# Gated linear attention and a maxout layer: small constants built on the chip, the output matrix read in 3 KB rows, and another order of the work

## The chip, the core and the metric

The kernel runs on one core of a Trainium2 chip. A core has TensorE (PE, with its weight loads shown as PEld), VectorE (DVE), ScalarE (ACT), GpSimd (POOL) and SyncE (SP), which here issues all DMA transfers. The metric is the device time of one execution in microseconds (us).

## The reference

Four batches of 8 heads, 768 tokens, head dimension 48. Each head carries a state of 48x48 from token to token; its rows are decayed by alpha, and the token's key and value are added. The result, 3072 rows of 384, goes through a layer that takes the largest of three products and multiplies it by an output matrix.

```python
for t in range(S):
    state = alpha[:, :, t, :, None] * state + einsum('bhd,bhe->bhde', k[:, :, t], v[:, :, t])
    y[:, :, t] = einsum('bhd,bhde->bhe', q[:, :, t], state)
x = y.transpose(0, 2, 1, 3).reshape(B * S, H * D)           # 3072 x 384
h = maximum(maximum(x @ w1, x @ w2), x @ w3)                # w: 384 x 768
out = h @ w_out                                             # w_out: 768 x 384
```

Inputs and output are float32.

## The kernel before

**Steps.** The work is cut into 12 steps of 256 tokens: step s is chunk s // 4 of batch s % 4. Of a step, partition p holds tokens 2j and 2j+1 of every head (U = 2 halves of J = 64 pairs, R = 2 tokens a pair). A state passes from step s to s + 4.

**One step, in pieces.** Each piece is a function, named by a letter in the order string; the number behind it is a part, then the engine (v DVE, p POOL, a ACT), then @step, and after # the PSUM banks.

- l0 to l3 (L100) load alpha, k, q, v of a step (384 KB each) into rings of four buffers (ra, rk, rq, rv). m (L204) multiplies the pair's two alphas; N (L207) takes the logarithm into la; r0 and r1 (L211) make the inverse decay inside the pair; u and w (L218, L221) bring k and q to the pair's end.
- c (L227) sums logarithms on PE with the triangular matrix upto and the two-column matrix pick; e, f, g (L243 to L249) turn the sums into factors ic, ac and the gates ge by exponentials.
- k and q (L262, L265) scale k and q into qk (float16), V (L268) scales v into vt, v (L273) copies halves of vt to vu.
- T with t (L279, L286) transposes qk on PE with the identity matrix and copies it out of PSUM; D (L289) does the same by DMA, for steps 5 to 11. A (L294) makes the scores, a (L312) masks them into lat with pmask, or with rowmask for step 0.
- Y (L366) applies scores and old state to the values, x (L369) copies the result to xT. S (L378) makes the step's addition to the state, s, M and z (L396, L373, L403) add and decay it, y (L408) spreads it to st.

**The layer.** The maximum is computed as w1 x plus the larger of 0, (w2-w1) x and (w3-w1) x. d (L416) makes the differences wdif in column groups of 256; b (L422) makes w1 in float16, B and n (L425, L431) transpose it, C (L434) makes w_out in float16, P and p (L437, L442) multiply w1 by w_out once into w1o. G (L445) makes the six products of a step with wdif (6 matmuls each), h (L455) takes their maximum into hT, O (L486 in project) multiplies xT by w1o and hT by w_out (9 matmuls), o (L493) scales by ys_c into ob, W (L497) stores.

**Weights in borrowed buffers.** K0 to K8 (L114) load 384 KB pieces of w1, w2, w3, the first eight into buffers 2 and 3 of the input rings; so l0@2, the load of step 2's alpha into ra2, must wait until d0, d1 and b0 have read K0 from it. K9 to K11 load w_out (L121) in rows of 1.5 KB.

**Constants.** Two matrices are computed on the host and loaded as J1 and J0 (L128): ca (34.5 KB: upto, pick and three columns of scales vs_c, ys_c, undo_c) and cb (64 KB: identity and pmask). I (L307) spreads pmask to rowmask.

**Padding.** Heads are 64 wide in las, qks, vts and vus but hold 48 columns; clear_padding (L145) zeroes the rest and the state buffers st: 16 memsets of st and 2 of la on DVE, 3 of vu, 4 of qk and 4 of vt on POOL.

**The order.** The program is one hand-held list, ORDER, which gives each engine its instructions in that order; no scheduler changes it. SP's queue takes loads, stores and DMA transposes in the same order, and one that has to wait holds up all behind it. H pieces (L505) are warm matmuls: products of a zero matrix that fill PE at the start; "H2^k0@1" begins with a small one that waits for the named result (L524). The list begins:

```python
l0@0 J1@0 l1@0 J0@0 l3@0 l0@1 r0a@0 m0v@0 l2@0 N0a@0 r1a@0 u0v@0 H15@0#0 c0@0#0 g0a@0 e0a@0 K0@0 f0a@0
k0v@0 l1@1 V0v@0 K2@0 H6@0#1 H1^k0@0#1 S0@0#1,2 K1@0 l2@1 I0a@0 r0a@1 m0p@1 l3@1 M0p@0 N0a@1 w0v@0 q0v@0
```

Of the kernel before, what the change touches and what calls it, by code (L numbers as in the profile page):

```python
# [23 lines left out]
def kernel(  # L24
# [101 lines left out]
    rowmask = cpool.tile([P, R, P], FP16, name="rowmask")  # L126

    def load_const(_, i, eng):  # L128
        c, c_np = ((ca, ca_np), (cb, cb_np))[i]
        queues[eng].dma_start(c, nc.inline_tensor(c_np, name=f"c{i}").ap())  # L130

    half = ca.bitcast(FP16)
    upto, pick = half[:, :P], half[:, P:P + 2 * U]
    c32 = ca[:, P // 2 + U:]
    ident, pmask = cb[:, :P], cb[:, P:2 * P]
    vs_c, ys_c, undo_c = c32[:, 0:1], c32[:, 1:2], c32[:, 2:3]
# [6 lines left out]
    sts = [[cpool.tile([P, HP, 2, D], FP16, name=f"st{b}_{i}") for i in range(2)] for b in range(B)]  # L143

    def clear_padding():  # L145
        for st in (st for pair in sts for st in pair):
            for i in range(2):
                nc.vector.memset(st[64 * i:64 * (i + 1), :, 1 - i], 0.0)
        for la in las:
            nc.vector.memset(la.rearrange("p r a b c -> p (r a b) c")[:, :, D:], 0.0)  # L150
        for vu in vus:
            nc.gpsimd.memset(vu.rearrange("p u a b c -> p (u a b) c")[:, :, D:], 0.0)
        for qk, vt in zip(qks, vts):
            nc.gpsimd.memset(qk.rearrange("p r i a b c -> p (r i a b) c")[:, :, D:], 0.0)
            nc.gpsimd.memset(vt.rearrange("p a b c -> p (a b) c")[:, :, D:], 0.0)


# [69 lines left out]
    def sums(s, *_):  # L227
# [79 lines left out]
    def spread_mask(_, i, eng):  # L307
        for u in range(U):
            for r in range(R):
                copy(eng, rowmask[u * J:(u + 1) * J, r], pmask[r * J:(r + 1) * J])  # L310

    def masked(s, x, eng):  # L312
# [103 lines left out]
    def differ(_, i, eng):  # L416
        jg, g = divmod(i, 2)
        engines[eng].tensor_sub(  # L418
            wdif[:, :, g, column_group(jg)], staged(3 * jg + 1 + g).rearrange("p (f j) -> p f j", f=NF),
            staged(3 * jg).rearrange("p (f j) -> p f j", f=NF))  # L420
# [101 lines left out]
    def warm_after(n, name):  # L522
# [5 lines left out]
        "l": load_step, "J": lambda _, i, eng: load_const(0, 1 - i, eng), "I": spread_mask, "K": load_weight, "H": warm,  # L528
# [9 lines left out]
    def emit(order):  # L538
# [12 lines left out]
        l0@0 J1@0 l1@0 J0@0 l3@0 l0@1 r0a@0 m0v@0 l2@0 N0a@0 r1a@0 u0v@0 H15@0#0 c0@0#0 g0a@0 e0a@0 K0@0 f0a@0  # L551
        k0v@0 l1@1 V0v@0 K2@0 H6@0#1 H1^k0@0#1 S0@0#1,2 K1@0 l2@1 I0a@0 r0a@1 m0p@1 l3@1 M0p@0 N0a@1 w0v@0 q0v@0
        H6@0#3 c0@1#3 l0@4 f0a@1 H1@0#4 T1@0#4 s0v@0 z0v@0 b0v@0 e0a@1 t1a@0 u0v@1 k0v@1 H1@0#5 B0@0#5 T0@0#6
        y0a@0 r1a@1 d1v@0 t0a@0 d0v@0 g0a@1 n0a@0 H1@0#7 H2^k0@1#7 H0^d1@0#7 A1@0#7,0 A0@0#1,4 w0v@1 l0@2 a2v@0
        K3@0 q0p@1 V0a@1 K4@0 a0v@0 K5@0 s1v@0 a3v@0 l1@2 H3@0#6 H2^a2@0#6 S0@1#6,3 s0a@1 m0p@4 a1v@0 v1a@1
# [5 lines left out]
        A1@2#5,4 V0a@2 l0@5 G4@0#0 a3v@2 a2v@2 A0@2#6,3 b2a@0 S0@2#2,1 M0p@4 M0p@2 G5@1#4 s0v@2 m0p@3 v1a@2
        a1v@2 l2@4 G4@1#5 a0v@2 z0p@2 h4a@0 v0v@2 y0a@2 G5@0#2 h1v@1 Y2@2#3 Y0@2#6 x0v@2 N0a@3 Y3@2 B2@0#0 l1@3
        x1a@2 c0@3#7 M1v@0 C2v@0 n2a@0 G4@2#6 G1@2#3 u0v@4 C0a@0 m0p@5 h5v@0 G3@2#0 l2@3 s1v@2 G2@2#2 C1v@0
        f0a@3 h4a@1 z1v@0 P0@0#1 h2v@2 h3v@2 P1@0#5 l3@4 k0p@4 N0a@5 h5v@1 r0a@3 P2@0#2 h4v@2 p0a@0 l3@3 r1a@3
        p1a@0 c0@5#0 p2v@0 G0@2#4 e0a@5 O1@0#6 h0a@2 g0a@5 w0v@4 q0v@4 e0a@3 T1@4#1 g0a@3 u0v@3 O0@1#5 o1a@0
        k0v@3 l0@7 y1a@0 l1@5 w0v@3 f0a@5 l0@8 r0a@5 q0v@3 T0@4#2 o0a@1 G5@2#4 t1a@4 M1v@1 V0v@4 l0@6 T0@3#7
        V0v@3 O0@0#6 t0a@3 h1v@2 v0p@3 l3@5 t0v@4 h5v@2 S0@4#0,5 v0p@4 o0a@0 S0@3#1,7 s0v@4 A0@4#3,2 s0v@3 l3@6
        T1@3#4 M0v@3 a1v@4 z0p@4 O0@2#6 l1@6 t1a@3 a0v@4 s1v@4 z0p@3 y0a@3 s1v@3 W1@0 m0p@7 A1@4#0,1 y0a@4
        A1@3#2,4 a2v@3 A0@3#3,5 a1v@3 O1@2#7 a3v@4 r0a@7 m0p@6 N0a@7 a3v@3 V0a@5 l2@5 u0p@5 c0@7#2 l2@6 O1@1#5
        N0a@6 r1a@5 a2v@4 v1p@3 l0@9 a0v@3 v1a@4 Y0@4#1 o1v@1 k0p@5 m0p@8 Y3@3#4 Y0@3#0 Y2@3 o0v@2 x0a@3 Y1@4  # L570
        W0@0 Y3@4#3 Y2@4 x1a@3 r0a@6 f0a@7 x0v@4 x1v@4 c0@6#5 G4@3#6 N0a@8 W0@2 w0v@5 G4@4#0 z1v@1 e0a@7 q0v@5
        f0a@6 r1a@6 w0p@6 D0@5 e0a@6 g0a@7 G0@4#4 h0a@4 G2@3#1 h2v@3 G3@3#3 V0a@6 r0a@8 G1@4#2 m0p@9 h4v@3 l2@7
        D1@5 c0@8#4 h3v@3 G5@3#1 q0p@6 g0a@8 N0a@9 h1v@4 G1@3#6 e0a@8 l1@7 o1v@2 c0@9#3 G0@3#2 h5v@3 M1p@4 g0a@6
        u0v@6 k0p@6 G2@4#7 r1a@7 h0v@3 f0a@9 G5@4#1 g0a@9 h1v@3 G3@4#5 v1a@5 h4a@4 h5v@4 O1@3#2 r0a@9 M1p@5 D0@6
        h2a@4 z1p@4 r1a@9 f0a@8 h3v@4 M0p@8 M0p@5 M1p@2 w0p@7 e0a@9 S0@5#6,0 D1@6 A0@5#1,7 y1a@1 s0v@5 A1@5#4,5
        a0v@5 a3v@5 O0@3#3 O1@4#6 z0p@5 v1a@6 W0@1 l3@7 s1v@5 z1p@2 v0a@5 M0p@6 a2v@5 M1p@3 u0p@7 l1@8 a1v@5
        y0p@5 l3@8 o1v@4 Y2@5#1 o0a@3 Y3@5 M0v@9 k0v@7 Y0@5#5 Y1@5 A1@6#0,4 x1a@5 S0@6#7,6 A0@6#3,1 x0a@5 s0v@6
# [58 lines left out]
```

## Time and profile before

| | |
|---|---|
| median of 3 runs | 142.0 us (141.97 to 146.79) |
| the profiled execution | 143.14 us |
| its span | 141.4 us |
| granted TensorE clock | 0.997 |
| instructions | 5309 |
| moved by DMA | 32.42 MB, mean 229 GB/s |

The profile shows one execution. Its page gives each engine's busy time, then the span in 40 slices of 3.5 us: a digit is the busy share in tenths. A row of the timeline is start, duration (of a merged run of instructions), engine, line, operation, output <- input, shapes and count; in brackets the idle time of that engine ahead of it and what ended it. A row of waits is the engine with the instruction that waited, what it waited for, the sum in us, the number of waits and the longest. SPq is SP's queue: its row lasts as long as issuing takes, waiting included.

### The profile page before, as it was taken

Reading aid. Unit: us, or ns where it says so; the run is one execution under the profiler, and the core shown is the slowest. Engines: PE = TensorE matmul, PEld = TensorE weight load, DVE = VectorE, ACT = ScalarE, POOL = GpSimd, SP = SyncE. Lnnn points to the kernel's source line nnn. Section 1 sums busy time; section 2 is a strip of 40 time slices with the busy share of each in tenths; the row PEclk is TensorE's granted clock in tenths of the full one; section 3 lists DMA queues with packets and bytes.
Section 4 is the critical chain, followed back from the end, with each engine's and each line's share of the span. In section 5 each row is a group of like instructions: output and inputs, shape, how many; then the busy total and the mean of one; then the engine's idle time right before and its main releaser. Section 6 shows DMA issues by size and latency. Waiting matters only on the chain.

```text
span 141.4 us, 5309 instructions
## 1 busy us (share of the span) xinstructions
PE 130.9 (93%) x2238; PEld 94.6 (67%) x2238; DVE 116.7 (83%) x220; ACT 96.0 (68%) x202; POOL 65.4 (46%) x102
## 2 busy tenths in 40 slices
PE   6977697999998999999998999999999999999990
PEld 2434265787865676688767867787567876788670
DVE  5559979998999998979797987979989899847511
ACT  3667689999974978999997734497657480554121
POOL 8230171268080059939892999458507501700000
PEclk9999999999999999999999999999999999999998
DMA  4999999999996299998999899999999859401433
GB/s 111 273 333 349 298 261 335 321 326 365 302 282 173 52 322 320 278 308 151 230 216 228 250 188 291 272 169 233 197 267 318 182 112 257 154 5 63 159 111 111
DMA packets 73031, 32.42 MB, mean 229 GB/s; under 512 B 65456, under 2 KB 73008, under 8 KB 73008
## 3 DMA queue, kind: packets, MB, share of 16 engines
q1 hardware_dynamic: 73008, 32.09, 88.3%
q8 instruction: 17, 0.28, 0.7%
q14 instruction: 6, 0.05, 0.1%
HBM read 23.69 MB, written 4.72 MB: 201 GB/s over the span
## 4 chain that ended last, share of the span: by engine, by line
PE 51%; DMA 16%; DVE 16%; SPq 6%; POOL 3%; ACT 3%; issue 2%; DVEq 0%
PE bank L452 22%; PE bank L486 17%; DMA ra<-in_alpha_dram 5%; PE bank L330 5%; DMA rv<-in_v_dram 4%; DMA qkT<-qk 4%; DMA rq<-in_q_dram 3%; SPq L102 3%; PE bank L304 3%; DVE lat L319 2%; PE bank L283 2%; DVE qk L260 2%; DVE hT L461 2%; SPq L290 2%; PE bank L388 2%
## 5 line engine op out<-in xcount | busy, mean ns | idle before, releaser
L452 PE MATMUL bank<-xT,wdif 128*128 128x256 f16 x432 | 51.5, 273 | 0.3 <-DVE wdif L418 0.3
L452 PEld LDWEIGHTS <-wdif 128*128 128x128 f16 x432 | 40.7, 98 | 6.5 <-DVE wdif L418 0.6
L319 DVE TENSOR_TENSOR lat<-bank,cb 128x512 f16<-128x512 f32 x44 | 27.8, 682 | 1.5 <-PE bank L304 1.5
L486 PE MATMUL bank<-wo,hT 128*128 128x384 f16 (+1 forms) x150 | 27.5, 320 | 0.0
L461 DVE TENSOR_TENSOR hT<-bank,h 128x512 f16<-128x512 f32 x36 | 23.8, 686 | 3.9 <-PE bank L452 2.1
L486 PEld LDWEIGHTS <-hT 128*128 128x128 f16 x150 | 14.5, 98 | 9.0
L465 ACT ACTIVATE h<-bank 128x512 f16<-128x512 f32 x20 | 11.7, 601 | 7.9 <-PE bank L452 7.9
L486 PE MATMUL bank<-w1o,xT 128*128 128x384 f16 (+1 forms) x75 | 15.9, 320 | 0.0
L168 ACT ACTIVATE ob<-bank,ca 128x384 f32<-128x384 f32 (+1 forms) x15 | 8.4, 572 | 10.8 <-PE bank L486 8.0
L205 POOL TENSOR_TENSOR ra<-ra 128x384 f32<-128x384 f32 x9 | 9.0, 999 | 11.1 <-DMA ra<-in_alpha_dram 10.8
L505 PE MATMUL bank<-hT 128*128 128x512 f16 x41 | 12.2, 420 | 1.2 <-DVE hT L603 1.2
L463 DVE TENSOR_SCALAR h<-bank 128x512 f16<-128x512 f32 x16 | 10.7, 685 | 3.1 <-PE bank L452 3.0
L162 ACT CAST st<-kept 64x192 f16<-64x192 f32 x28 | 9.7, 347 | 4.9 <-POOL kept L404 4.7
L164 POOL COPY vu<-vt 64x384 f16<-64x384 f16 x16 | 8.0, 502 | 9.6 <-DVE vt L170 8.9
L162 ACT COPY vu<-vt 64x384 f16<-64x384 f16 x24 | 12.2, 509 | 0.4
L260 POOL TENSOR_TENSOR qk<-rq,ac 128x768 f16<-128x768 f32 x5 | 9.1, 1816 | 7.2 <-DVE rq L222 7.1
L260 POOL TENSOR_TENSOR qk<-rk,ic 128x768 f16<-128x768 f32 x5 | 9.4, 1877 | 2.3 <-DVE rk L219 1.6
L162 ACT CAST xT<-bank 128x384 f16<-128x384 f32 x14 | 6.3, 479 | 5.7 <-PE bank L330 5.7
L222 POOL TENSOR_TENSOR rq<-rq,ic 128x384 f32<-128x384 f32 x6 | 6.0, 1002 | 7.7 <-ACT ic L216 7.7
L304 PE MATMUL bank<-qkT 48*64 48x128 f16 x384 | 8.6, 219 | 0.7 <-DMA qkT<-qk 0.4
L170 DVE TENSOR_SCALAR ob<-bank,ca 128x384 f32<-128x384 f32 (+1 forms) x10 | 5.8, 591 | 3.8 <-PE bank L486 3.8
L168 ACT ACTIVATE vt<-rv,ca 128x768 f16<-128x768 f32 x8 | 7.5, 935 | 2.0 <-DMA rv<-in_v_dram 1.9
(82 smaller groups left out, 214.3 us busy)
## 6 DMA issues: line engine op xcount, KB each, us to landing
ra<-in_alpha_dram SPq DMA_DIRECT2D x12, 384.0 KB, 5.3
rk<-in_k_dram SPq DMA_DIRECT2D x12, 384.0 KB, 5.2
rv<-in_v_dram SPq DMA_DIRECT2D x12, 384.0 KB, 5.6
rq<-in_q_dram SPq DMA_DIRECT2D x12, 384.0 KB, 4.8
out_dram<-ob SPq DMA_DIRECT2D x23, 192.0 KB, 2.2
wst<-in_moe_w_out_dram SPq DMA_DIRECT2D x3, 384.0 KB, 6.1
ra<-in_moe_w_dram SPq DMA_DIRECT2D x2, 384.0 KB, 5.2
rk<-in_moe_w_dram SPq DMA_DIRECT2D x2, 384.0 KB, 6.2
```

Source lines behind the costliest of these rows:

```text
L162: nc.scalar.copy(out=dst, in_=src)
L168: nc.scalar.mul(dst, src, col)
L205: engines[eng].tensor_mul(raw("a", s, 0), raw("a", s, 0), raw("a", s, 1))
L260: engines[eng].tensor_mul(dst, src, by)
L304: nc.tensor.matmul(aps[i][to * J:(to + 1) * J, a * U + n, :], qkT[rows, r, 1, p, cols], qkT[rows, :, 0, p, cols], start=True, stop=True)
L319: nc.vector.tensor_mul(lats[s % 2][u][:, i], bank(("aps", s, u, i), [HP, P]), pmask.unsqueeze(1).broadcast_to([P, HP, P]))
L452: nc.tensor.matmul(gps[:, j, :], wdif[:, f, g, jj * P:(jj + 1) * P], xT[:, f].rearrange("p u t -> p (u t)"), start=(f == 0), stop=(f == NF ...
L461: nc.vector.tensor_max(hTs[s % NH][:, 2 * jg:2 * jg + 2, :], gps, h)
L463: nc.vector.tensor_scalar_max(h, gps, 0.0)
L465: nc.scalar.activation(out=h, in_=gps, func=AFT.Relu)
L486: nc.tensor.matmul(ops, lhs, (w1o if what == "x" else wo16)[:, j, cols], start=((what, j) == every[0]), stop=((what, j) == every[-1]))
L505: nc.tensor.matmul(wps, blank[:, :P], blank, start=True, stop=True)
```

## The change

- The transfers ca and cb go. make_sums builds upto (POOL: iota, memset, affine select; DVE: one memset and two additions of -1 on blocks), make_masks builds the identity and pmask on POOL, make_scales builds pick and the three columns by small DVE instructions and one ACT exponential.
- Zeroing: the eight state buffers become one tile, spread, cleared by two DVE memsets. The padding of vu and of vt2, vt3 is cleared by ACT copies from a zero buffer (blank), that of qk0, qk1, vt0, vt1 stays on POOL, that of qk2 (ACT) and qk3 (DVE) comes later as piece Z.
- w_out is loaded with two neighbouring rows on a partition (3 KB rows). The columns of the maxout layer are then permuted to match: d and b write their outputs with neighbouring source columns 128 columns apart.
- ORDER is a new list. It loads and sums the alpha of step 1 ahead of step 0's, and it moves pieces between engines. By counts of the two lists: h 52 to 49 on DVE and 20 to 23 on ACT; z 8 to 2 on DVE and 12 to 18 on POOL; o 10 to 6 on DVE and 15 to 19 on ACT; k 7 to 5 on DVE and 5 to 7 on POOL; V 4 to 2 on DVE and 8 to 10 on ACT; t 3 to 5 on DVE and 7 to 5 on ACT; m 3 to 6 on DVE and 9 to 6 on POOL; y 14 to 11 on ACT, 6 to 8 on POOL, 0 to 1 on DVE. PE's pieces are as many as before; the warm matmuls are 43 and one small one (41 and 4 before).

```diff
-    ca = cpool.tile([P, P // 2 + U + 3], FP32, name="ca")
-    cb = cpool.tile([P, 2 * P], FP16, name="cb")
-        queues[eng].dma_start(c, nc.inline_tensor(c_np, name=f"c{i}").ap())
-                                  moe_w_out.rearrange("(j p) m -> p j m", p=P)[:, 2 * (i - 9):2 * (i - 8)])
+                                  moe_w_out.rearrange("(g p j) m -> g p j m", p=P, j=2)[i - 9])
...
+    def make_sums():
+        nc.gpsimd.iota(place_of, [[0, 1]], base=0, channel_multiplier=1)
+        nc.gpsimd.memset(ones, 1.0)
+        nc.gpsimd.affine_select(upto, ones, [[1, P]], AOP.is_ge, 0.0, base=0, channel_multiplier=-1)
+        nc.vector.memset(upto[:J, J:], 0.0)
+        for u in range(U):
+            block = upto[u * J:u * J + J // 2, u * J:(u + 1) * J]
+            nc.vector.tensor_scalar_add(block, block, -1.0)
+    def make_scales():
+        nc.vector.memset(pick, 0.0)
...
+        nc.vector.tensor_single_scalar(place_in[:, 0:1], place_of, J - 1, AOP.bitwise_and)
+        nc.vector.tensor_single_scalar(place_in[:, 1:2], place_of, P - R, AOP.bitwise_and)
+        nc.vector.tensor_scalar(vs_c, place_in[:, 0:1], R * LAM, at + SIGMA, AOP.mult, AOP.add)
+        nc.vector.tensor_scalar(ys_c, place_in[:, 1:2], -LAM, -at - SIGMA, AOP.mult, AOP.add)
+        nc.scalar.activation(out=c32[:, 0:2], in_=c32[:, 0:2], func=AFT.Exp)
+    def make_masks():
+        nc.gpsimd.affine_select(ident, ones, [[1, P]], AOP.is_equal, 0.0, base=0, channel_multiplier=-1)
...
+            nc.scalar.copy(out=vu.rearrange("p u a b c -> p (u a b) c")[:, :, D:], in_=zeros[:, :U * H])
...
-            wdif[:, :, g, column_group(jg)], staged(3 * jg + 1 + g).rearrange("p (f j) -> p f j", f=NF),
+            wdif[:, :, g, column_group(jg)].rearrange("p f (j n) -> p f n j", j=2), staged(3 * jg + 1 + g).rearrange("p (f n j) -> p f n j", f=NF, j=2),
...
-        l0@0 J1@0 l1@0 J0@0 l3@0 l0@1 r0a@0 m0v@0 l2@0 N0a@0 r1a@0 u0v@0 H15@0#0 c0@0#0 g0a@0 e0a@0 K0@0 f0a@0
+        l0@1 l0@0 l1@0 l3@0 Z2a@0 m0v@1 N0a@1 r0a@1 H10@0#0 c0@1#0 e0a@1 f0a@1 l2@0 K1@0 K0@0 K2@0 r1a@1 r0a@0
+        l1@1 l3@1 m0v@0 N0a@0 H8@0#1 c0@0#1 g0a@0 M0v@0 l2@1 u0v@0 l0@4 f0a@0 e0a@0 k0v@0 V0a@0 r1a@0 H8@0#2
+        S0@0#2,3 s0v@0 I0a@0 b0a@0 w0p@0 q0v@0 H6@0#4 T1@0#4 d0v@0 g0a@1 t1a@0 d1v@0 l0@2 M0v@1 z0v@0 K3@0
+        T0@0#5 t0a@0 H2@0#6 H3^d1@0#6 A1@0#6,7 K4@0 B0@0#1 u0v@1 k0v@1 V0v@1 H1@0#2 S0@1#2,0 v0a@1 w0v@1 a2v@0
+        A0@0#4,5 a0v@0 y0a@0 r0a@4 s0a@1 r1a@4 H4@0#6 Y3@0#6 K5@0 s1v@0 a3v@0 l1@2 l2@2 K6@0 q0p@1 T1@1#4 v1v@1
+        t1a@1 T0@1#2 a1v@0 Y0@0#3 m0p@2 N0a@2 t0v@1 A1@1#7,4 c0@2#5 x0a@0 a3v@1 x1a@0 G0@0#2 K7@0 d2v@0 G2@0#3
+        b1a@0 z0p@1 m0p@4 N0a@4 d3v@0 l3@2 n0v@0 h0a@0 y0a@1 e0a@2 K8@0 c0@4#4 f0a@4 a2v@1 H1@0#6 A0@1#6,1 a1v@1
+        f0a@2 a0v@1 u0p@2 h2a@0 K11@0 l0@3 K9@0 B1@0#2 G3@0#7 h3v@0 r0a@2 r1a@2 Y3@1#1 Y0@1#6 x0v@1 Y2@1 x1a@1
...
-        o1v@10 W1@10 O6@11 o1v@11 W1@11 o2a@11 W2@11
+        h4a@11 h5v@11 o0v@10 W0@10 O3@11 o0v@11 W0@11 O4@11#6,2 o1v@10 W1@10 O6@11 o2a@11 W2@11 O5@11 o1a@11
+        W1@11
...
     with tc.manual_schedule():
         nc.vector.memset(blank, 0.0)
+        clear_states()
+        make_sums()
+        make_masks()
         clear_padding()
+        make_scales()
         emit(ORDER)
```

More of the change, by code (lines that the diff above doesn't have):

```diff
@@ new lines, in make_scales @@
+    def make_scales():
+        nc.vector.memset(pick, 0.0)
+        for u in range(U):
+            for i in range(2):
+                nc.vector.memset(pick[u * J + i * J // 2:u * J + (i + 1) * J // 2, u, i:i + 1], 1.0)
+        nc.vector.memset(undo_c, -LAM * P / 2)
+        at = LAM * (R - 1 - MID)
+        nc.vector.tensor_single_scalar(place_in[:, 0:1], place_of, J - 1, AOP.bitwise_and)
[3 more added lines that the diff above has]
+        nc.scalar.activation(out=c32[:, 0:2], in_=c32[:, 0:2], func=AFT.Exp)
@@ L138 @@
+    def make_masks():
+        nc.gpsimd.affine_select(ident, ones, [[1, P]], AOP.is_equal, 0.0, base=0, channel_multiplier=-1)
+        for r in range(R):
+            rows = slice(r * J, (r + 1) * J)
+            nc.gpsimd.affine_select(pmask[rows], ones[rows].rearrange("p (r j) -> p r j", r=R),
+                                    [[r, R], [1, J]], AOP.is_ge, 0.0, base=-r, channel_multiplier=-1)
     las = [cpool.tile([P, R, HP, 2, 64], FP16, name=f"la{i}") for i in range(2)]
@@ L309, in spread_mask @@
             for r in range(R):
-                copy(eng, rowmask[u * J:(u + 1) * J, r], pmask[r * J:(r + 1) * J])
+                copy(eng, rowmask[u * J:(u + 1) * J, r], pmask[r * J:(r + 1) * J].rearrange("p r j -> p (r j)"))
     def masked(s, x, eng):
@@ L550 @@
     ORDER = """
[L551 to L555, printed above, removed]
@@ L561 @@
[L561 to L565, printed above, removed]
```

151 lines of the change are left out of this document (76 added, 75 removed).

## The prediction

> **What bounds the kernel now.** I read the page's sums and slices first, then PE's waits, then the timeline of the first 25 us engine by engine (SP's queue too), and last the timeline of the end.
>
> ```profile
> PE 130.9 (93%) x2238; PEld 94.6 (67%) x2238; DVE 116.7 (83%) x220; ACT 96.0 (68%) x202; POOL 65.4 (46%) x102
> ...
> PE   6977697999998999999998999999999999999990
> ...
> DMA  4999999999996299998999899999999859401433
> ```
>
> PE is full from about 25 us to the end, so the body is PE's own work, which the change leaves as it is. Before that PE has holes, and much of its busy time is filler: the warm matmuls (L505) have 12.2 us in the groups. DMA is full from 2 to 42 us.
>
> ```profile
> PE bank L440 <- DVE h L463: 0.7, 1, 0.7
> ...
> PE bank L304 <- DMA qkT<-qk: 0.4, 1, 0.4
> ```
>
> These are PE's longest waits after 25 us. By the table of windows PE idles 0.31 us in 25 to 30, 0.89 in 40 to 50, 0.39 in 70 to 80 and 0.17 in 100 to 110: these 1.8 us are all that a better order can win in the body. The rest is won or lost at the start and at the end.
>
> ```profile
> 4.10 0.31 POOL L155 MEMSET vt<- 128x256 f16 x1
> ...
> 4.34 0.52 ACT L214 ACTIVATE ic<-ra 128x384 f32<-128x384 f32 x1 [2.33 <-DMA ra<-in_alpha_dram]
> ...
> 5.00 0.52 ACT L209 ACTIVATE la<-ra 128x384 f16<-128x384 f32 x1
> ...
> 8.85 0.52 ACT L214 ACTIVATE ic<-ra 128x384 f32<-128x384 f32 x1 [0.48 <-DMA ra<-in_alpha_dram]
> 8.90 1.00 POOL L205 TENSOR_TENSOR ra<-ra 128x384 f32<-128x384 f32 x1 [4.49 <-DMA ra<-in_alpha_dram]
> ...
> 12.11 4.50 SPq L102 DMA_DIRECT2D ra<-in_alpha_dram  x2
> ...
> 24.86 0.96 DVE L418 TENSOR_TENSOR wdif<-rq,rv 128x768 f16<-128x768 f32 x1
> ```
>
> Step 0's alpha lands at 4.34 and its logarithms start at 5.00; step 1's alpha lands at 8.85. POOL does nothing between its last memset (4.41) and 8.90. The last difference of weights that step 0's gates need (d3, 24.86) ends at 25.82, and the gate behind it (G3@0) runs from 25.88 to 26.71. From there PE is full, so the end of G3@0, with what PE has done by then, measures the start.
>
> **The sum's base.** The profiled execution took 143.14 us with a span of 141.4 (1.7 around it). The median of the runs shown is 142.0. I work out a difference to the span and add it to the median.
>
> **The start.** Removed: the transfers ca and cb, 98.5 KB. The first 40 us move 297 GB/s, so what follows lands 0.3 us earlier, and SP is spared 0.56 + 0.92 us of issuing. Both are hidden if the chain below ends later; if it does not, they are worth 0.3.
>
> Added ahead of the first logarithm, which I call S. ACT is free at 2.01 (table load); five pad copies of 256 elements, between the rowmask copy (128 elements, 0.29) and the vu copy (384, 0.51), take 0.40 each, to 4.0. DVE: blank to 1.13; two memsets of 768 words (96 words 0.138, 128 words 0.165, 256 words 0.272, so 0.84 ns a word: 0.70 each) to 2.6; two la memsets 0.33; 14 small ones of 0.10 (POOL's one-element memset) to 0.16 (DVE's gm) each: done at 4.3 to 5.1. Then ACT's Exp (as ge, 0.29) and the pads of qk2 (512 elements as h, 0.60): S is 5.2 to 6.0. Step 1's product on DVE (0.53) is done by then. I take 5.5.
>
> POOL makes upto: from 0.73 an iota (0.10 to 0.20 by the small memset and gm), ones (0.2 to 0.3) and a select, which no row shows: at least a memset of 128 (0.15), at most POOL's two-input rate (1.0 for 384: 0.35 plus 0.1). Upto is there at 1.2 to 1.8, DVE asks at 2.6: taken as hidden. The masks behind it (three selects, under 1.5 us) and four pads (1.7) end by 5.5 and are asked for after 13.
>
> From S, with the distances of the same rows: Ln to the first Exp 1.25, each ACT pass 0.37 to 0.42. Step 1's two Exps and inverse, then step 0's Ln (S+2.8), its sums on PE, three Exps to S+5.1. Scaling k (0.96) to 6.1, values (ACT 0.94) 5.9, inverse 6.4, near_q on POOL (1.0) 7.4, scaling q 8.4. Two transposes and two ACT copies (1.0 each) to 11.1, scores (0.65) 11.8. DVE beside it: d0, d1 (0.9 each) to 10.1, gm and kept 10.6, step 1's near_k, k, values, near_q (0.5, 0.9, 0.6, 0.55) 13.1; step 1's q on POOL (1.8) 14.9, transposes to 16.0. DVE meanwhile: a2, a0, fb, a3, vu, a1, the copy of step 1's transposes to 17.0. Y0@0 (0.74) and A1@1 (0.65) on PE to 17.8, a3 of step 1 18.4, d2 19.3, d3 20.25. PE then has G2@0, c0@4, A0@1 and B1@0 (0.65, 0.4, 0.46, 0.34) to 21.2 and ends G3@0 at S+21.85 = 27.35, against 26.71: 0.65 later, but with B1@0 (0.34) done, which stood behind it. Then DVE has n0v, a2, a1, a0 of step 1 (0.5, 0.6, 0.6, 0.65) to 22.6, and Y0@1 waits for the last one 0.55 us. **Start: +0.9.**
>
> Queues moved past: l0@2 refills the buffer of the first weights, so SP stands at it until d1v@0. Now it stands in the row at 12.11 until 16.6 (d1v ends 16.22); then it would go at S+10.1 = 15.6, and the weights for d3 (landed 24.86) come about 0.9 earlier, at 24.0, ahead of S+19.3 = 24.8. Step 1's q comes after step 1's v instead of ahead of it: from 16.4 (issue 9.91 plus 6.5) to about 17.6, asked for at S+12.5 = 18.0. Near, but hidden. l0@4 waits for u0v@0 and step 0's Ln, about 10, when DMA has 6 transfers queued: nothing.
>
> w_out in 3 KB rows has the same 1.15 MB, landing behind a full DMA; its casts are as many: nothing. The new order of weight columns makes six differences and three halvings write with a stride. No row shows that. The nearest, xT (read with a stride, 0.55 for 384), goes at the plain rate: I take nothing, at most a doubling (0.95 each for d0 to d3, +3.8).
> [...]
>
> **The body.** Counted over the two orders at the rows' durations, DVE has 7.0 us less, ACT 4.9 more (besides the pads), POOL 4.1 more. The waits that DVE ends (0.7, 0.3) should go, those on a transfer or ACT stay: from 1.8 to 1.2, **-0.6**, between -1.8 and +1 (what a single transfer wait costs now, 0.4, two or three times).
>
> **The end.** Now the last two halves are scaled side by side, DVE 137.80 and ACT 137.97, 0.42 each. Then both are ACT's: the second starts as the first ends, about 138.2. **+0.2.**
>
> Sum: +0.9 - 0.6 + 0.2 = +0.5, so 142.5.
>
> **Rivals.**
> POOL comes late (slower). In both kernels POOL's list has an unnamed ISA instruction ahead of its first operation that is no plain memset; in the kernel before that is ahead of L205, and it lies in the hole from 4.41 to 8.85, which the alpha's landing ends. What it costs is hidden: 0 to 4.45 us, call it x. In the new kernel it stands ahead of the iota, DVE's queue stands at upto, and behind it all small constants, the Exp and S. About 1.1 is free (2.6 against 1.5), so the time is 142.5 + x - 1.1: 145.9 at the most, over 2% from x = 3.4. For it: the hole; against: 8.90 follows the landing by 0.05 only, and no transfer of code is seen before 12 us. 0.20.
> [...]
>
> ACT becomes the bound between 25 and 70 us: it has 5.4 us idle there now (0.3, 0.45, 2.7, 1.75, 0.15), up to G5@3 it is given 4.2 more, and it starts late by the pads. Should it run over, PE waits as long: 143.5 to 146. 0.12.
>
> Strided writes cost: up to 146.3. 0.06.
>
> Faster: the chain above overlaps better than I walk it, so that d3 follows its transfer (24.0, G3@0 0.9 earlier), and all the body's waits go: 142.0 - 0.9 - 1.8 + 0.2 = 139.5. 0.10.
>
> **How the numbers follow.** The forecast, 141.2 to 143.6, has 0.52. Within 2% of 142.0 (about what a measurement of this kernel can tell from no change) is 139.2 to 144.8. Slower: 0.11 of the POOL rival, 0.06 of ACT's, 0.05 of the strides, 0.02 of the forecast, 0.24. Faster: half of its rival and 0.02, 0.07. Same 0.69. The range 140.2 to 145.6 leaves out about 0.06 below and 0.13 above.
>
> **What would show it.** Right: upto before 2.6, first Ln near 5.5, G3@0 ending near 27.3, then PE idle under 1.5 us, the last ACT pass near 0.2 after its forerunner's place. POOL's rival: a hole ahead of the iota, with DVE waiting for POOL. ACT's: PE waits ended by ACT between 30 and 70. Strides: d0 above 0.96. Wrong would be a first Ln after 7, or PE idle over 3 us after 27.

## The result and the profile after

The changed kernel takes 160.69 us (median of 4, 160.19 to 161.61) against 141.99 us for the kernel before on the same chip: a ratio of 1.1355, 95% interval 1.1274 to 1.1437. Forecast were 142.5 us and a range of 140.2 to 145.6. It is 18 us slower than forecast, far outside the range, and the case that came true is the one that had a chance of 0.06 and a limit of 146.3. The profiled execution took 160.19 us, with a span of 158.5 and a mean granted TensorE clock of 0.957. Some executions of one and the same kernel take 1.5% or more above its fastest (146.79 us of the kernel before is one), and the ratios leave these out, so they differ a little from the quotients of the medians.

The page of the changed kernel, its sums and slices (a slice is 3.96 us here):

```profile
PE 134.9 (85%) x2237; PEld 96.8 (61%) x2237; DVE 124.0 (78%) x207; ACT 109.2 (69%) x215; POOL 73.4 (46%) x108
...
PE   6777079534994998799999999999999999999991
...
PEclk9999857995699999999999999999999999999999
DMA  4999259902993899699369999998997959534114
```

The first 14 slices, up to 55 us, hold nearly all of the loss: PE has holes in slices 5, 8 to 10 and 13, DMA has its own in 5, 9, 10 and 13, and the clock is low in 5 to 7 and in 10 and 11, in and behind PE's holes. Behind slice 14 only slices 16 and 17 (8 and 7) stand out against the line of the kernel before.

The start of the changed kernel, from its timeline:

```profile
0.90 0.13 POOL L115 IOTA place_of<- 128x1 int32 x1 [0.39 <-POOLq L640]
...
1.25 0.29 POOL L117 TENSOR_SCALAR_AFFINE_SELECT upto<-ones 128x128 f16<-128x128 f16 x1
...
2.94 0.09 DVE L118 MEMSET upto<- 64x32 uint32 x1
...
5.77 0.52 ACT L225 ACTIVATE la<-ra 128x384 f16<-128x384 f32 x1
```

POOL stands 0.39 us ahead of the iota and has upto at 1.54; DVE asks for it at 2.94. The first logarithm, the forecast's S, is at 5.77.

Then the weights. These rows are VectorE's (L434 makes the differences), ScalarE's (L178 casts w1 to float16, into ob) and GpSimd's, each from its own timeline:

```profile
12.76 3.62 ACT L178 CAST ob<-ra 128x768 f16<-128x768 f32 x1
...
13.62 3.56 DVE L434 TENSOR_TENSOR wdif<-rq,ra 128x768 f16<-128x768 f32 x1
...
16.79 3.78 DVE L434 TENSOR_TENSOR wdif<-rk,ra 128x768 f16<-128x768 f32 x1
...
30.43 3.55 DVE L434 TENSOR_TENSOR wdif<-ra,rv 128x768 f16<-128x768 f32 x1
33.60 3.78 DVE L434 TENSOR_TENSOR wdif<-rq,rv 128x768 f16<-128x768 f32 x1
...
43.97 3.65 POOL L434 TENSOR_TENSOR wdif<-rv,rk 128x768 f16<-128x768 f32 x1
47.23 3.79 POOL L434 TENSOR_TENSOR wdif<-wst,rk 128x768 f16<-128x768 f32 x1
```

Each of these had the same operands and the same count of elements before, at 0.95 to 0.96 us on DVE and 1.81 to 1.85 on POOL. Only where the results are written has changed. The four on DVE are 10.9 us longer together (14.67 against 4 x 0.95). Each overlaps the row behind it by some 0.4 us, so DVE's list falls a little less behind: from the start of a pair to that of the row behind it are 6.56 and 6.57 us, and 1.74 and 1.73 where all is plain (e2 below), 9.7 us in all.

PE's longest waits, and SP's queue:

```profile
PE bank L540 <- DVE gm L393: 5.4, 1, 5.4
PE bank L468 <- DVE wdif L434: 2.9, 1, 2.9
PE bank L468 <- POOL wdif L434: 2.4, 2, 1.9
PE bank L320 <- DVE w1T L180: 2.3, 1, 2.3
```

```profile
12.46 8.56 SPq L81 DMA_DIRECT2D ra<-in_alpha_dram  x2
```

The first wait, 5.4, is that of the warm matmul "H3^d1", which stands in PE's list until d1 is done (16.79 + 3.78 = 20.57; gm is the next small row on DVE). 2.9 and 2.3 are the gate behind d2 and the copy that DVE makes only after d3; 2.4 is POOL's d4 and d5. The row of SP is l0@2: it must not overwrite the buffer of K0 before d0 and d1 have read it, and so all later loads stand behind it until 21.0.

What happens to the clock, from the changed kernel's table of windows (2 us each; PE, PEld, DVE, ACT, POOL, granted clock, DMA share, GB/s):

```profile
16.00:18.00 2.00, 0.00 (x0) 0.00 (x0) 2.00 (x2) 2.00 (x4) 0.00 (x0) 1.00 0.32 88
18.00:20.00 2.00, 0.00 (x0) 0.00 (x0) 2.00 (x1) 0.14 (x1) 0.00 (x0) 0.64 0.00 0
20.00:22.00 2.00, 1.38 (x4) 0.29 (x3) 1.97 (x5) 0.00 (x0) 0.00 (x0) 0.50 0.10 20
22.00:24.00 2.00, 2.00 (x40) 1.28 (x43) 1.81 (x4) 1.20 (x3) 0.71 (x1) 0.50 1.06 314
24.00:26.00 2.00, 2.00 (x52) 1.00 (x44) 1.01 (x3) 1.68 (x5) 2.00 (x2) 0.66 1.01 340
```

PE is idle from 15.3 to 20.6 us, and then works at a granted clock of 0.50 until about 25.4 (an estimate: two thirds of the last row, whose mean is 0.66). So the matmuls behind this wait are slower too: the 16 of L320 at 22.03 take 0.65 us, at the full clock (29.28) 0.42. What that costs the kernel is the question of e9. DMA carries nothing from 18 to 20 us.

To see where the time is lost, I added up from each trace the columns that the matmuls move (the warm ones left out; the whole is the same in all kernels) and read off when a given share of them had been started. The table gives the time for the kernel before, and by how much each other kernel is later; the kernels are those of the next section. Each line is one execution: the profiled one of the kernel before took 143.14 us, 1.1 above its median, and that of e5 was the fastest of its four, so differences of 1 to 2 us at the end of a line say little.

| share of the matmul work | 5% | 10% | 20% | 25% | 50% | 99.9% |
|---|---|---|---|---|---|---|
| before, us | 20.4 | 27.5 | 40.0 | 49.6 | 77.6 | 137.6 |
| changed | +8.5 | +13.7 | +16.5 | +16.9 | +17.1 | +17.1 |
| changed, plain writes (e1) | +2.3 | +2.0 | +1.6 | +2.8 | +3.2 | +3.6 |
| the same once more (e1 again) | +3.7 | +2.6 | +2.2 | +2.6 | +3.2 | +2.3 |
| new order alone (e5) | +2.8 | +1.6 | +1.6 | +2.5 | +3.1 | +2.5 |
| new constants alone (e4) | -0.5 | -1.0 | +0.2 | -1.4 | -1.8 | -2.0 |

Up to 20% of the work, 56.5 us, the changed kernel has lost 16.5 us, up to 25% 16.9, and after that next to nothing.

### The profile page after: what moved, and what is told of

It is laid out like the page before. It is cut to its first block, busy times and chain, and to the rows that moved or that the text cites. A ratio compares the mean times of both kernels' runs of the same rounds, so it can differ in the third digit from the quotient of the medians.

```text
span 158.5 us, 5318 instructions
## 1 busy us (share of the span) xinstructions
PE 134.9 (85%) x2237; PEld 96.8 (61%) x2237; DVE 124.0 (78%) x207; ACT 109.2 (69%) x215; POOL 73.4 (46%) x108
## 4 chain that ended last, share of the span: by engine, by line
PE 45%; DVE 15%; POOL 9%; issue 9%; ACT 8%; DMA 7%; SPq 4%; ACTq 0%; POOLq 0%; DVEq 0%
PE bank L468 17%; PE bank L502 15%; POOL wdif L434 4%; DVE wdif L434 4%; PE bank L346 4%; DMA rk<-in_k_dram 4%; DMA rq<-in_q_dram 4%; SPq L81 3%; POOL qk L276 3%; PE bank L320 3%; PE bank L404 2%; DVE rq L238 1%; PE bank L299 1%; POOL rq L238 1%; DVE hT L477 1%
## 5 line engine op out<-in xcount | busy, mean ns | idle before, releaser
L468 PEld LDWEIGHTS <-wdif 128*128 128x128 f16 x432 | 41.3, 99 | 12.4 <-DVE wdif L434 3.2
L335 DVE TENSOR_TENSOR lat<-bank,pmask 128x512 f16<-128x512 f32 x44 | 28.1, 682 | 4.7 <-PE bank L320 4.6
L502 PE MATMUL bank<-wo,hT 128*128 128x384 f16 (+1 forms) x150 | 27.5, 320 | 0.0
L184 ACT ACTIVATE ob<-bank,c 128x384 f32<-128x384 f32 (+1 forms) x19 | 10.4, 563 | 14.6 <-PE bank L502 10.7
L276 POOL TENSOR_TENSOR qk<-rq,ac 128x768 f16<-128x768 f32 x6 | 11.3, 1881 | 19.0 <-DVE rq L238 14.1
L502 PEld LDWEIGHTS <-hT 128*128 128x128 f16 x150 | 14.5, 98 | 8.9
L481 ACT ACTIVATE h<-bank 128x512 f16<-128x512 f32 x23 | 13.9, 610 | 7.2 <-PE bank L468 7.0
L276 POOL TENSOR_TENSOR qk<-rk,ic 128x768 f16<-128x768 f32 x7 | 13.7, 1954 | 9.9 <-ACT ic L256 9.9
L178 ACT COPY vu<-vt 64x384 f16<-64x384 f16 x28 | 14.2, 508 | 5.0 <-DVE vt L186 4.6
L521 PE MATMUL bank<-hT 128*128 128x512 f16 x43 | 13.7, 459 | 1.3 <-DVE hT L619 1.3
L178 ACT CAST xT<-bank 128x384 f16<-128x384 f32 x14 | 6.5, 478 | 8.8 <-PE bank L346 8.7
L320 PE MATMUL bank<-qkT 48*64 48x128 f16 x384 | 9.7, 230 | 2.3 <-DVE w1T L180 2.3
L521 PEld LDWEIGHTS <-hT 128*128 128x128 f16 x43 | 4.3, 113 | 11.9 <-issue 8.7
L320 PEld LDWEIGHTS <-qkT 48*64 48x64 f16 x384 | 6.8, 112 | 5.4 <-issue 4.9
L420 POOL TENSOR_TENSOR kept<-fa,gm 128x192 f32<-128x192 f32 x10 | 5.2, 523 | 9.1 <-DVE fa L416 8.8
L184 ACT ACTIVATE vt<-rv,c 128x768 f16<-128x768 f32 x10 | 9.4, 939 | 0.1
L178 ACT CAST spread<-kept 64x192 f16<-64x192 f32 x22 | 7.6, 347 | 2.0 <-POOL kept L420 1.7
```

The costliest lines, as they stand in the source:

```text
L178: nc.scalar.copy(out=dst, in_=src)
L184: nc.scalar.mul(dst, src, col)
L276: engines[eng].tensor_mul(dst, src, by)
L320: nc.tensor.matmul(aps[i][to * J:(to + 1) * J, a * U + n, :], qkT[rows, r, 1, p, cols], qkT[rows, :, 0, p, cols], start=True, stop=True)
L468: nc.tensor.matmul(gps[:, j, :], wdif[:, f, g, jj * P:(jj + 1) * P], xT[:, f].rearrange("p u t -> p (u t)"), start=(f == 0), stop=(f == NF ...
L481: nc.scalar.activation(out=h, in_=gps, func=AFT.Relu)
```

## The experiments

My theory after the result (A): the strided float16 writes are the loss, by their own length and by what waits for them. The rival (B): the new order, or the constants, lose it, and the long rows are only where it shows. The kernels ran on several chips; the ratio is always to the kernel before on the same chip (medians 143.44 us beside e1 to e4, 141.98 beside e5, e7, e8 and e10, 142.43 beside e9, e11 and the repeats).

**e1: the changed kernel without the rows and the strides.**

```diff
-                                  moe_w_out.rearrange("(g p j) m -> g p j m", p=P, j=2)[i - 9])
+                                  moe_w_out.rearrange("(j p) m -> p j m", p=P)[:, 2 * (i - 9):2 * (i - 8)])
...
-            wdif[:, :, g, column_group(jg)].rearrange("p f (j n) -> p f n j", j=2), staged(3 * jg + 1 + g).rearrange("p (f n j) -> p f n j", f=NF, j=2),
+            wdif[:, :, g, column_group(jg)], staged(3 * jg + 1 + g).rearrange("p (f j) -> p f j", f=NF),
```

> The changed kernel with w_out again in 1.5 KB rows and its columns in order, so that differences and halvings write contiguously; constants on the chip and the new order stay. Theory A (the strided float16 writes are the cause: 3.6 to 3.8 us each where the kernel before has 0.82 to 1.85): the nine operations fall back to 0.95 (DVE), 0.82 (ACT), 1.8 (POOL), and the time to 142.5 us (141 to 144). Rival B (the new order loses the time, whatever the writes): over 150 us.

146.49 us, ratio 1.0215 (1.0132 to 1.0298); profiled span 145.0, clock 0.999. The first difference, d0, is plain again:

```profile
13.64 0.95 DVE L434 TENSOR_TENSOR wdif<-rq,ra 128x768 f16<-128x768 f32 x1
```

So of the 18.7 us 14 (by the medians) to 16 (by the ratios, 0.114 x 142) are the rows and strides, and the clock's fall goes with them. The rest, 3 us by the ratio, theory A did not foresee.

**e2: the 3 KB rows kept, the writes contiguous, the stride on the reading side.**

```diff
-            wdif[:, :, g, column_group(jg)].rearrange("p f (j n) -> p f n j", j=2), staged(3 * jg + 1 + g).rearrange("p (f n j) -> p f n j", f=NF, j=2),
+            wdif[:, :, g, column_group(jg)].rearrange("p f (j n) -> p f j n", j=2), staged(3 * jg + 1 + g).rearrange("p (f n j) -> p f j n", f=NF, j=2),
```

> The changed kernel with 3 KB rows kept, but differences and halvings walk the columns in the order of the output: contiguous float16 writes, float32 reads 8 bytes apart. Theory A1 (only the write's stride costs): each operation within 10% of its contiguous time, and the time within 1% of the kernel with plain rows, about 142.5 us. Rival A2 (a stride costs on either side): operations at 3 us or more and about 160 us.

147.93 us (145.77 to 148.67; no interval came with it), span 145.8. The same permutation of columns, written in order and read with a step of 8 bytes (VectorE's d0 and GpSimd's d4):

```profile
13.62 0.95 DVE L434 TENSOR_TENSOR wdif<-rq,ra 128x768 f16<-128x768 f32 x1
...
31.28 2.16 POOL L434 TENSOR_TENSOR wdif<-rv,rk 128x768 f16<-128x768 f32 x1
```

All four differences on DVE take 0.95 us again and the cast on ACT 0.89 to 0.91 (0.82 before); only POOL's two, 2.16 against 1.82, are more than the 10% dearer that A1 allowed. The time is 1% over e1's, but not the 142.5 us expected, as in e1. It is the writing, not the permutation and not the 3 KB rows.

**e3: the kernel before, with the rows and the strided writes alone.** The edit is the reverse of e1's, made in the kernel before.

> The kernel before with the 3 KB rows and the strided writes alone; constants and order are the old ones. Theory A: four differences on DVE at 2.7 us more and a halving on DVE at 3 us more stand in the chain of the start, and the load behind the first differences goes later: 154 to 161 us. Rival B (the new order is what makes it dear): under 148 us.

164.03 us, ratio 1.1468 (1.1375 to 1.1562), span 163.6, clock 0.927. The strides alone, without new order or constants, cost at least as much as the whole change does (the two intervals overlap), and more than I expected. In the old order the first cast (b0) is DVE's too, so DVE has five such operations ahead of 41 us instead of four. From its timeline:

```profile
13.10 3.54 DVE L164 CAST ob<-ra 128x768 f16<-128x768 f32 x1
...
18.00 3.56 DVE L418 TENSOR_TENSOR wdif<-rk,ra 128x768 f16<-128x768 f32 x1
21.17 3.78 DVE L418 TENSOR_TENSOR wdif<-rq,ra 128x768 f16<-128x768 f32 x1
...
12.92 12.44 SPq L102 DMA_DIRECT2D ra<-in_alpha_dram  x2
```

d1 ends at 24.95, and SP stands at l0@2 for 12.4 us instead of 8.6. The more of these operations lie ahead of d1, the longer all loads wait. The strided rows also stretch others: VectorE's product of q at 43.37 takes 3.45 us instead of 0.55, to 46.82, beside GpSimd's d5 (4.19 from 42.73, to 46.92); in the changed kernel one product meets d5 (49.46, of alphas), and it takes 1.47.

**e10 and e12: which writes are dear?** Behind the last store, VectorE and ScalarE run single operations in turn, with at most each other beside them (the kernels' own times say nothing). All read float32.

> Old order, constants on the chip, plain rows; behind the last store DVE subtracts and ACT copies 768 float32 elements a partition into a scratch buffer with several patterns, each by itself: contiguous float16; float16 in two streams 256 bytes apart (as in the change); 258 bytes apart; single float16 4 bytes apart; two streams 8 bytes apart; float32 in two streams 512 bytes apart; contiguous float16 with reads 8 bytes apart. The times are read per instruction, the whole time says nothing. Theory A3 (every float16 that does not follow its neighbour costs about 4.6 ns): the four scattered float16 patterns take about 3.6 us on both engines, float32 and contiguous ones 0.8 to 1.0. Rival A4 (the distance of 256 bytes is what costs): 258, 4 and 8 bytes at about 1 us, float32 512 bytes apart slow too.

> The changed kernel with plain rows and writes; behind its last store VectorE and ScalarE each run ten operations on their own, one after the other (the kernel's own time says nothing). All read float32. 768 float16 elements: contiguous; written in two streams 8, 16 and 64 bytes apart; written contiguously but read in two streams 512 bytes apart. 192 float16 elements: contiguous, with a step of 8 and of 16 bytes. 192 float32 elements: contiguous, with a step of 16 bytes. Theory L (a write that goes to another piece of 16 bytes than the write before it pays): 8 bytes apart 0.95 on VectorE and 0.83 on ScalarE as before; 16 and 64 bytes apart 3.55; a step of 8 bytes no more than 0.1 us above contiguous, a step of 16 bytes dear by some 3.6 ns an element, 0.7 us more. Theory M (only jumps over a long distance, or back and forth, pay): 16 bytes apart and the steps are plain, 64 bytes apart lies between. For the read over 512 bytes there is no row: by L it is as dear as the write if reading works as writing does, plain if only writing pays.

VectorE's rows of e10, in order: contiguous; float16 in two streams 256 bytes apart; 258 bytes apart; one stream with a step of 4 bytes; two streams 8 bytes apart; float32 in two streams 512 bytes apart; written contiguously, read with a step of 8 bytes.

```profile
135.95 0.95 DVE L640 TENSOR_TENSOR rq<-rk,rv 128x768 f16<-128x768 f32 x1
137.79 3.55 DVE L642 TENSOR_TENSOR rq<-rk,rv 128x768 f16<-128x768 f32 x1 [0.90 <-ACT rq L641]
144.98 3.54 DVE L644 TENSOR_TENSOR rq<-rk,rv 128x768 f16<-128x768 f32 x1 [3.64 <-ACT rq L643]
152.15 1.01 DVE L646 TENSOR_TENSOR rq<-rk,rv 128x768 f16<-128x768 f32 x1 [3.63 <-ACT rq L645]
154.27 0.96 DVE L648 TENSOR_TENSOR rq<-rk,rv 128x768 f16<-128x768 f32 x1 [1.11 <-ACT rq L647]
155.14 1.50 DVE L650 TENSOR_TENSOR ra<-rk,rv 128x768 f32<-128x768 f32 x1
156.49 0.94 DVE L652 TENSOR_TENSOR rq<-rk,rv 128x768 f16<-128x768 f32 x1
```

So neither the permutation (0.96 written in two streams 8 bytes apart, 0.94 read with that step) nor a step of 4 bytes (1.01) is dear, and two more bytes of distance change nothing (3.54 against 3.55): A3, which had steps of 4 and 8 bytes dear as well, and A4 are both wrong. In e12 the streams are 8, 16 and 64 bytes apart (L650, L652, L654); L656 writes in order and reads in two streams 512 bytes apart; then 192 float16 elements contiguous, with a step of 8 and of 16 bytes, and last 192 float32 elements with a step of 16 bytes.

```profile
138.23 0.96 DVE L650 TENSOR_TENSOR rq<-rk,rv 128x768 f16<-128x768 f32 x1 [0.90 <-ACT rq L649]
140.08 3.56 DVE L652 TENSOR_TENSOR rq<-rk,rv 128x768 f16<-128x768 f32 x1 [0.90 <-ACT rq L651]
147.30 3.57 DVE L654 TENSOR_TENSOR rq<-rk,rv 128x768 f16<-128x768 f32 x1 [3.66 <-ACT rq L653]
154.54 0.97 DVE L656 TENSOR_TENSOR rq<-rk,rv 128x768 f16<-128x768 f32 x1 [3.67 <-ACT rq L655]
156.57 0.36 DVE L658 TENSOR_TENSOR rq<-rk,rv 128x192 f16<-128x192 f32 x1 [1.06 <-ACT rq L657]
157.35 0.58 DVE L660 TENSOR_TENSOR rq<-rk,rv 128x192 f16<-128x192 f32 x1 [0.42 <-ACT rq L659]
158.62 1.01 DVE L662 TENSOR_TENSOR rq<-rk,rv 128x192 f16<-128x192 f32 x1 [0.68 <-ACT rq L661]
...
160.89 0.50 DVE L666 TENSOR_TENSOR ra<-rk,rv 128x192 f32<-128x192 f32 x1 [1.08 <-ACT ra L665]
```

For two streams the edge lies between 8 and 16 bytes (0.96 and 3.56), and at 64 bytes it is no dearer (3.57): L, not M. But a step of 8 bytes costs more than L expected (0.22 us): what fits these rows is not the distance, but how often the writing moves to another piece of 16 bytes. With 768 such moves a row takes 3.56 us, with 192 (the step of 16 bytes) 1.01: 2.55 us for 576 moves, or 4.4 ns a move, which leaves 0.16 us for the rest of a row. An estimate by these two numbers meets the other float16 rows: 192 moves for the 768 elements with a step of 4 bytes give 1.01 (measured 1.01), 96 moves for the 192 elements with a step of 8 bytes 0.58 (0.58). Two streams 8 bytes apart have only 96 moves for 768 elements, by the same estimate 0.58 us, less than the 0.95 that 768 elements take in order, and the row took 0.96: as if a row took the longer of the two.

Reading over 512 bytes costs VectorE nothing measurable (0.97 against 0.95). ScalarE goes the same way: 0.83 contiguous, 3.59 and 3.60 at 16 and 64 bytes, 1.04 with a step of 4 bytes, 1.00 for the read. Float32 is no such case: on VectorE 192 elements with a step of 16 bytes took 0.50, and 0.56 contiguous. Why float16 pays and float32 hardly does, these runs do not show.

**e9: is the halved clock a part of the loss?**

```diff
-        T0@0#5 t0a@0 H2@0#6 H3^d1@0#6 A1@0#6,7 K4@0 B0@0#1 u0v@1 k0v@1 V0v@1 H1@0#2 S0@1#2,0 v0a@1 w0v@1 a2v@0
+        T0@0#5 t0a@0 H16@0#6 H3^d1@0#6 A1@0#6,7 K4@0 B0@0#1 u0v@1 k0v@1 V0v@1 H1@0#2 S0@1#2,0 v0a@1 w0v@1 a2v@0
```

> The changed kernel whole, with 16 warm-up matmuls instead of 2 in the hole that TensorE has while it waits for l0@2's and d1's work, before the last warm-up that waits for d1. In the changed kernel the granted clock is 0.50 to 0.66 from 20 to 26 us, behind a hole of some 5 us. Theory C (the halved clock behind each hole is a good part of the loss): the hole is filled for about 3 of its 5 us, the clock from 20 to 26 us comes back near 1, and the time falls by 1 to 3 us, to 158 to 159.7. Theory A (the strided differences on VectorE end each stretch, and TensorE waits for them whatever its clock): the clock may come back, but TensorE then waits longer for d2 and d3, and the time stays within 0.5 us of 160.7.

159.09 us, ratio 1.1178 (1.11 to 1.1255), on another chip than the changed kernel's 1.1355 (1.1274 to 1.1437). By the ratios it gains about 1.6%, as theory C wants; its profiled execution has the same span (158.6 against 158.5) and clock (0.956). The windows of e9:

```profile
18.00:20.00 2.00, 0.28 (x2) 0.00 (x1) 2.00 (x1) 0.14 (x1) 0.00 (x0) 1.00 0.00 0
20.00:22.00 2.00, 1.34 (x23) 0.71 (x23) 1.97 (x5) 0.00 (x0) 0.00 (x0) 0.94 0.05 10
22.00:24.00 2.00, 2.00 (x56) 1.31 (x55) 1.84 (x4) 1.17 (x3) 0.68 (x1) 0.50 1.01 291
```

The hole is now 2.4 us long, and the clock still halves, only later. So the experiment did not do what it was made for, and what the clock alone costs stays open. In this trace e9 leads the changed kernel by 1.2 us at 5% of the work and by 0.3 at 25%: PE does its work earlier, and then waits for the same d2 and d3.

**e4, e5, e8: the other parts alone.** e4 is the kernel before with the constants made on chip and the zeroing of the change; e5 the kernel before with the new list ORDER; e8 is e4 with the 3 KB rows, and writes as in e2.

> Constants made on the chip with the old order (without the two loads of constants, with the two late paddings ahead of the first logarithm) and plain rows. Theory A: the first logarithm goes from 5.0 to about 6.2 us behind ACT's paddings, so 142 to 143.5 us. Rival C (making constants on the chip costs more than its chain, on POOL or by contention): over 144.5 us.

> The code of the kernel before (constants loaded, plain rows, paddings cleared at the start) with the new order alone; the two loads of constants stand behind the first two loads. Theory D (the new order itself loses the remaining 4 us, by DVE and POOL meeting in time): 145 to 147 us against 146.5 with constants made on the chip. Rival C (the new order is only slow together with constants made on the chip): 143.5 us or less.

> Old order, constants on the chip, and w_out in 3 KB rows with contiguous writes (the reads go 8 bytes apart). Theory F (the rows of w_out land behind a full DMA and are worth nothing): within 0.7 us of the same kernel with plain rows, 142.5 us, and 0.3 to 1.5 us under the kernel before. Rival G (longer rows pay once the writes are contiguous): under 141.5 us.

e4: 142.51 us, ratio 0.9936 (0.9886 to 0.9985). e5: 147.39 us, 1.0341 (1.026 to 1.0423). e8: 142.12 us, 0.9977 (0.9935 to 1.002). The constants with the zeroing gain 0.6% at most: e8, which has them too, cannot be told from the kernel before. That is the only gain found here, and e4 the best version by a hair. The 3 KB rows gain nothing as theory F has it. The new order loses 2 to 4%, with the old constants (e5, a little above the 145 to 147 us expected) as with the new (e1). So what remains in e1 is the order's.

**e7 and e11: what does the new order lose?** In e1, VectorE and GpSimd multiply float32 pairs at the same time between 45 and 50 us. VectorE's rows of e1 there:

```profile
45.19 1.36 DVE L238 TENSOR_TENSOR rq<-rq,ic 128x384 f32<-128x384 f32 x1
46.47 2.16 DVE L235 TENSOR_TENSOR rk<-rk,ra 128x384 f32<-128x384 f32 x1
48.55 1.75 DVE L276 TENSOR_TENSOR qk<-rq,ac 128x768 f16<-128x768 f32 x1
```

With no GpSimd product beside them the same operations take 0.55, 0.55 (e7's rows below) and 0.95 us (a product of k at 50.22 in e1), so the three rows are 0.8, 1.6 and 0.8 us longer; GpSimd's three rows beside them last from 44.97 to 49.49. PE waits 2.6 us for the result (1.9 in the changed kernel). e7 takes e1 and moves two of GpSimd's three to VectorE; e11 moves two more such pieces (u0@2, u0@4).

```diff
-        w0v@4 u0v@3 c0@5#6 G3@2#4 G5@2#5 w0p@3 q0p@3 O0@1#1 q0v@4 T0@4#0 l0@6 k0v@3 l2@6 l0@7 h5v@2 s1v@2 T1@4#7
+        w0v@4 u0v@3 c0@5#6 G3@2#4 G5@2#5 w0v@3 q0v@3 O0@1#1 q0v@4 T0@4#0 l0@6 k0v@3 l2@6 l0@7 h5v@2 s1v@2 T1@4#7
```

> The changed kernel with plain rows, and step 3's near_q and scaling of q on DVE instead of POOL, so that POOL is quiet while DVE makes its own products between 45 and 50 us. DVE gets 1.5 us more work. Theory D (DVE's three products of 0.55, 0.55 and 0.96 us take 5.27 us there because POOL's products run beside them): they fall back to their plain times, PE's longest wait (2.6 us for a scaled k or q) falls under 1.5, and the time to 144 to 145.5 us. Rival E (DVE simply has too much listed there): PE's wait grows, 146.5 us or more.

> The changed kernel with the output matrix in its old rows and contiguous writes, once more, beside the next two on one chip. Ratio to the kernel before 1.02 to 1.03, as in its first run (1.0215): about 145 to 146.5 us.

> The kernel of the run above with w0@3 and q0@3 on VectorE instead of GpSimd, on the same chip. If the meeting of two-input products of VectorE and GpSimd from 45 to 50 us is what the new order loses (theory D1), the time falls by 1.5 to 2.5 us under the run above, to a ratio of 1.005 to 1.015. If it is only one of several places, each of which takes over when another goes (theory D2), it falls by 0.3 to 1.3 us, and TensorE's waits turn up elsewhere (for the decay's logarithms and for a difference of the weights).

> The kernel of the run above, with u0@2 and u0@4 (the two scalings of k that GpSimd still does beside VectorE's difference d3 and its product of k) on VectorE as well. Theory D1: d3 and the product of k fall from 1.75 to 0.95 us, TensorE's wait of 1.1 us for d3 goes, and the time falls by another 0.5 to 1.5 us, to a ratio of 1.00 to 1.01. Theory D2: VectorE now has 1.1 us more of its own work in the stretches where it is the fullest engine, and the time moves by less than 0.5 us either way.

e7: 144.74 us, 1.0202 (1.0133 to 1.0271); that lies in the range expected in us, but on a chip where the kernel before took 141.98, and the ratio is e1's. On one chip: e1 again 145.5 us, 1.0222 (1.0162 to 1.0282); e7 again 145.48 us, 1.0186 (1.0113 to 1.0259); e11 149.05 us, 1.0459 (1.0378 to 1.054). In e7's trace the place is mended:

```profile
45.16 0.55 DVE L238 TENSOR_TENSOR rq<-rq,ic 128x384 f32<-128x384 f32 x1
45.62 0.55 DVE L235 TENSOR_TENSOR rk<-rk,ra 128x384 f32<-128x384 f32 x1
46.09 0.55 DVE L238 TENSOR_TENSOR rq<-rq,ic 128x384 f32<-128x384 f32 x1
```

though the next product of k (48.49) takes 1.75; GpSimd's next product in the list is u0@5. At 25% of the work e7 is 1.1 us behind the kernel before where e1 is 2.8; yet the whole gains at most 0.4%, inside the intervals. e11 is clearly slower than e7, the two intervals lie apart, which neither D1 nor D2 had. The difference that GpSimd's u0@2 had stretched (d3 in e1, d2 in e7, 1.76 each) is plain again (0.95), but k of step 2 now has to wait for VectorE, and GpSimd with it:

```profile
28.96 1.81 POOL L276 TENSOR_TENSOR qk<-rk,ic 128x768 f16<-128x768 f32 x1 [6.40 <-DVE rk L235]
31.08 0.21 POOL L393 TENSOR_TENSOR gm<-ge,ge 128x4 f32<-128x4 f32 x1 [0.31 <-ACT ge L266]
31.24 2.61 POOL L434 TENSOR_TENSOR wdif<-rv,rk 128x768 f16<-128x768 f32 x1
```

GpSimd idles 6.4 us, starts the product at 28.96 instead of 27.00 in e7, and its work then falls beside VectorE's scalings of q at 29.8 to 32.2. The meeting has only moved. So theory D1, that the meetings are what the order loses, falls: the one at 45 to 50 us is real and costs PE time there (its longest wait for a scaled k or q is 2.6 us in e1 and 0.9 in e7), but is not the whole, and emptying GpSimd makes VectorE, already 93 to 99% busy from 20 to 50 us in e1, the later one. What stays open is the rest of the order's loss: 1.6 and 2.2 us are lost in e1's two traces by 20% of the work, before the meeting, and no single place was found for them.

## Why the prediction was wrong, point by point

**The step that failed** is "The nearest, xT (read with a stride, 0.55 for 384), goes at the plain rate: I take nothing, at most a doubling (0.95 each for d0 to d3, +3.8)." The measured factor is 3.7 to 4.0 on VectorE (3.55 to 3.78 against 0.95), 4.4 on ScalarE (3.62 against 0.83) and 2.0 on GpSimd (3.65 to 3.79 against 1.82). Three things were wrong in it. The nearest row was of another kind: xT reads with a stride, and reading with one costs VectorE nothing measurable here (e12, 0.97 against 0.95), writing does: 4.6 ns an element (3.55 us / 768), where contiguous writes take 1.2 (0.95 us / 768). "At most a doubling" had no row at all behind it, so as an upper end it was a guess. And the sum took only d0 to d3's own length, when their lateness is paid again: 10.9 us of longer rows on VectorE (9.7 by the starts of what follows them) became 13.5 us (changed against e1: +17.1 against +3.6 at the end; 14.8 against e1's repeat), with POOL's two rows, SP's queue and the halved clock behind them; how these share the other 3 to 5 us was not separated.

**The start, "+0.9".** Its parts on the small constants were right: upto at 1.54 (1.2 to 1.8 forecast), S at 5.77 (5.2 to 6.0, taken 5.5), DVE free for upto at 2.94 (2.6). With plain writes, d0 starts at 13.64 (forecast S + 8.3 = 13.8) and l0@2 goes when d1 ends: SP's row in e1 runs from 12.50 to 15.90 (15.6 forecast). But G3@0 ends at 28.93 in e1, forecast 27.35. 0.8 us of that is d3, stretched beside GpSimd's u0@2 from 0.95 to 1.76, which the walk through the list did not see, because it priced each engine's rows alone.

**The body, "-0.6".** The order does not win the waits back. From 20% of the work to its end e1 loses another 2.0 us (3.6 against 1.6), 1.2 of them up to 25%; its repeat loses 0.1 (2.3 against 2.2), e5 0.9. So the sign was taken wrong, and the bound of +1 held in two of the three traces.

**The end, "+0.2".** From 99.9% of the matmul work to the end of the span it is 3.8 us in both kernels: nothing measurable.

**The rivals.** POOL late: wrong, it idles 0.39 us ahead of the iota. ACT the bound between 25 and 70 us: not seen, the rows of PE in e1 between 30 and 70 us name no wait that ACT ends. Strided writes: right in kind, at a quarter of the size. The sentence of the prediction by which this was to be recognised, "d0 above 0.96", was the right one: 3.56.

Without the strides the forecast of 142.5 would still have been 2.6 us low: e1's ratios, 1.0215 and 1.0222, make 145.0 and 145.1 us of 141.99, inside the range that ends at 145.6. But that the range would have held is luck: 0.5 us of loss was forecast and 3.1 came, the body's sign was wrong, and the meetings of VectorE and GpSimd stood in no term.

## What to carry to other kernels

Where a layout is permuted, put the stride on the reading side and write in order (VectorE's differences took 0.95 us so, and 3.55 to 3.78 with the stride on the writing side); if writing must be strided in float16, count how often it moves to another piece of 16 bytes: here that took 4.4 ns each time, and only with four or eight writes to a piece was it hidden or nearly so (0.96 us against 0.95 with eight, 1.01 with four, but 0.58 against 0.36 with two). A price that no row shows has no upper end, above all for an operation that others wait for: what stands behind it (here a refill and all loads behind that) is paid as well. And a row's length holds for the neighbours it had: before two-input products are moved, look at what the other of VectorE and GpSimd does at that time (a VectorE product of 0.55 us took 2.16 in e1).

## What the runs showed of the hardware

- In float16 writes 768 moves to another piece of 16 bytes took 3.54 to 3.60 us on VectorE and on ScalarE at distances of 16, 64, 256 and 258 bytes, and 192 moves 1.01 and 1.04: about 4.4 ns a move. Two streams 8 bytes apart are plain (0.96 and 0.83 for 768); single writes 8 bytes apart are not (0.58 against 0.36, and 0.62 against 0.35, for 192). That a row takes its moves or its plain time, whichever is longer, is an estimate from these rows.
- By the windows of 2 us, the granted clock was 0.50 for 6.8 us in the changed kernel (an estimate from the rows, 18.6 to 25.4), where PE was idle for 5.4 us (15.3 to 20.6), and for 3.4 us in e9 (21.8 to 25.2), where PE had been idle for 2.4 us and then at work for 1.1 (from 20.66). What sets when the clock falls and for how long, these runs do not show.
- One VectorE product with two inputs took 2.16 us instead of 0.55 beside GpSimd products (e1), and 3.45 beside a strided GpSimd difference (e3).
